# A long convolution and a SwiGLU block on one core: folded transforms, spectra kept on chip, transposes by DMA

## The chip, the core and the metric

The kernel runs on one core of a Trainium2 chip. The core has TensorE (PE, matrix products), VectorE (DVE), ScalarE (ACT), GpSimd (POOL) and SyncE (SP, here only a queue of DMAs), each with its own list of instructions that it takes in order; they meet through semaphores. 16 DMA engines move data between HBM and SBUF. The metric is the device time of one execution in microseconds (us), lower is better. Before the change it is 398.52 us, the median of three runs (397.84 to 399.33).

## The reference

The input has 2048 rows (time) of 640 channels, in bf16. Layer A is a gated long convolution, layer B a SwiGLU feed-forward block with 1728 hidden channels, each with a layer norm ahead and a residual:

```python
    k_shift = sum_t k_pad[:, t:t + S, :] * shift_k[:, ks - 1 - t]     # 4 taps
    kv = k_shift * v
    y = causal_conv(kv, ssm_k)          # rfft of length 2S, product, irfft; 2048 taps a channel
    y = y + kv * ssm_D
    A = q * y                           # q = layernorm(x)
    h = x + A
    g = silu(layernorm(h) @ w_gate);  u = layernorm(h) @ w_up
    out = h + (g * u) @ w_down
```

(`causal_conv` stands for the three FFT lines of the reference.)

## The kernel before, in words

Time is cut into four blocks of 512 rows. The convolution of a block is done by a real transform of 1024 coefficients (512 cosines, 512 sines at odd half frequencies), held as a matrix of constants: the transform is a matrix product on PE. A spectrum is a tile of 128 partitions x 8 x 640 (8 coefficient tiles; 0 to 3 the cosine half, 4 to 7 the sine half).

- `g_piece(p)` loads 512 taps of the filter (640 channels on partitions), transposes them on PE (L196) through PSUM, copies them out (L197), transforms them (`fwd_transform`, L153, 64 products of 128x128 by 320 columns, and eight copies L155), and for p > 0 combines piece p with piece p-1 by sign vectors (`hbuild`, L179 and L181). The combined spectra of p = 1 to 3 go to DRAM (`hf_dram`), and so do the raw ones of p = 1 and 2 (`graw_dram`); `pair` fetches the first kind again.
- `conv_front_tiles(j)` loads 128 rows of x, of k at four shifts and of v on SP's queue, takes the sum and the sum of squares of x on ACT (L124, L125), and computes `kv` on DVE (L257 to L262, eight operations of 640 columns per 128 rows). `conv_front_finish` normalises x on ACT (L139) and transforms `kv` into `Xcur` (64 products, L153).
- `pair(j, pp)` multiplies `Xcur` by the filter spectrum pp and adds it into the accumulator of block j+pp: six or eight DVE operations of 2560 columns (`cmac`, L162 to L176). There are ten pairs.
- `conv_back(j)` makes the inverse transform (L303, 64 products), multiplies by the normalised x (L306), adds x (L313, loaded a second time), stores h to DRAM, takes the statistics of h, normalises it on ACT (L139), transposes it on PE (L335) and copies it into `hlnT` (L336).
- `ffn_quarter(q)` runs over 14 chunks of 128 hidden channels: five products of 512 columns for the gate (L356), five for the up part (L358); ACT takes the sigmoid (L360), and copies gate (L362) and up (L364) out of PSUM; DVE multiplies twice (L366, L367). Then `ps_mm<-wd_sb,tT` (L376, 112 products of 320 columns) and, per 128 rows, the residual (L381) from h, which POOL's queue loads again, and the store. The weights of gate and up come in groups of two chunks on POOL's queue (L346, L348) for every quarter.
- `ln_finish_block` forms 1/std by an ACT square root (L134) and a DVE reciprocal (L135).

The Tile layer turns this program into one list per engine. It orders each list by the priority of the instructions (their place in the program if nothing else is said) and by its own estimate of when operands are there, and sets the semaphore waits. So the filter pieces, the front of the next block and the feed-forward block of the last one are interleaved on each engine; once built, each list is fixed.

## Time and profile before

| what | us |
|---|---|
| median of three runs | 398.52 |
| span of the profiled execution, first to last instruction | 397.7 |
| PE busy (share) | 325.7 (82%) |
| DVE busy | 254.7 (64%) |
| ACT busy | 253.8 (64%) |
| POOL busy | 68.1 (17%) |
| first product of the convolution starts at | 25.9 |
| last feed-forward block starts at about | 346 |

The profiled execution is one execution of the same program; its span lies 0.8 us under the median of the runs, and the difference is what lies around the first and last instruction. In the views, L12 is line 12 of the kernel; `out<-in xN | busy, mean` gives the busy time of a group in us and the mean of one instruction in ns; what stands behind the second bar is the idle time of the engine before the group and what ended it. A row of a timeline starts with its start and its length in us. "PEclk" is the clock that the throttle granted to PE, 1.00 being full.

### The profile page before, as it was taken

The numbers are of one execution on the slowest core, as the hardware profiler recorded it, in microseconds if no ns is written. First come the engines' busy times: TensorE is split into PE (matmuls) and PEld (weight loads), VectorE is DVE, ScalarE is ACT, GpSimd is POOL, SyncE is SP. The second block draws the span as 40 slices with busy tenths as digits, with TensorE's granted clock in tenths as the row PEclk, the third lists the DMA queues.
The fourth block names the chain that finished last, engine by engine and source line by source line (L and its number), as shares of the span: only waits on it lengthen the run. The fifth ranks groups of instructions, "written<-read, shape, count | busy, mean of one in ns | idle before, by whom it ended". The sixth has DMA issues, their size and how long they took to land.

```text
span 397.7 us, 5429 instructions
## 1 busy us (share of the span) xinstructions
PE 325.7 (82%) x1914; PEld 185.3 (47%) x1936; DVE 254.7 (64%) x413; ACT 253.8 (64%) x447; POOL 68.1 (17%) x95
## 2 busy tenths in 40 slices
PE   1038874497899779999779899897998999999995
PEld 1025542364567324565354355454534554544463
DVE  1185498500629989999949999983699723233321
...
GB/s 249 180 314 357 296 146 242 157 66 109 321 303 259 356 335 218 101 178 220 305 190 101 266 49 199 104 155 56 16 141 106 112 96 77 100 155 142 52 51 49
DMA packets 33610, 68.91 MB, mean 173 GB/s; under 512 B 4213, under 2 KB 25904, under 8 KB 31920
## 3 DMA queue, kind: packets, MB, share of 16 engines
...
HBM read 56.77 MB, written 11.80 MB: 172 GB/s over the span
## 4 chain that ended last, share of the span: by engine, by line
PE 33%; issue 25%; ACT 14%; DMA 13%; DVE 11%; SPq 2%; POOL 2%; POOLq 0%; DVEq 0%; ACTq 0%
PE ps_g L356 11%; PE ps_mm L376 7%; PE ps_mm L153 6%; PE ps_u L358 6%; PE ps_mm L303 4%; DMA wu_g<-in_B_w_up_dram 3%; ACT gc L362 3%; ACT xln_blk L139 3%; DMA k_148<-in_A_k_dram 2%; DMA wg_g<-in_B_w_gate_dram 2%; ACT junk L124 2%; SPq L250 2%; ACT sig L360 2%; DMA WF_t<-const_wf 1%; DMA wbig<-in_A_shift_k_dram 1%
## 5 line engine op out<-in xcount | busy, mean ns | idle before, releaser
L356 PE MATMUL ps_g<-hlnT,wg_g 128*128 128x512 bf16 (+1 forms) x268 | 70.9, 386 | 11.1 <-DMA wg_g<-in_B_w_gate_dram 6.1
L153 PEld LDWEIGHTS <-WF_t 128*128 128x128 bf16 x512 | 51.3, 101 | 48.7 <-DMA WF_t<-const_wf 13.8
L358 PE MATMUL ps_u<-hlnT,wu_g 128*128 128x512 bf16 (+1 forms) x270 | 70.3, 384 | 2.0 <-ACT uc L364 1.3
L376 PE MATMUL ps_mm<-wd_sb,tT 128*128 128x320 bf16 x448 | 69.6, 302 | 1.0 <-DVE tT L367 1.0
L360 ACT ACTIVATE sig<-ps_g 128x512 bf16<-128x512 f32 (+1 forms) x56 | 33.4, 597 | 50.0 <-PE ps_g L356 44.5
L376 PEld LDWEIGHTS <-tT 128*128 128x128 bf16 x448 | 41.9, 98 | 25.6 <-issue 7.1
L346 POOL DMA_DIRECT2D wg_g<-in_B_w_gate_dram x28 | 24.4, 873 | 168.9 <-PE ps_g L356 156.2
L153 PE MATMUL ps_mm<-gT,WF_t 128*128 128x320 bf16 x256 | 40.8, 313 | 15.1 <-DMA WF_t<-const_wf 13.5
L356 PEld LDWEIGHTS <-wg_g 128*128 128x128 bf16 (+1 forms) x280 | 27.3, 99 | 47.4 <-issue 14.7
L153 PE MATMUL ps_mm<-kv_blk,WF_t 128*128 128x320 bf16 x256 | 39.0, 307 | 6.9 <-ACT Xcur L155 3.9
L358 PEld LDWEIGHTS <-wu_g 128*128 128x128 bf16 (+1 forms) x280 | 27.5, 99 | 34.6 <-issue 3.7
L366 DVE TENSOR_TENSOR gs<-gc,sig 128x512 bf16<-128x512 bf16 (+1 forms) x56 | 23.2, 419 | 30.3 <-ACT gc L362 30.3
L364 ACT CAST uc<-ps_u 128x512 bf16<-128x512 f32 (+1 forms) x56 | 32.8, 586 | 10.8 <-DVE tT L367 3.3
L303 PEld LDWEIGHTS <-WI_t 128*128 128x128 bf16 x256 | 25.8, 102 | 17.5 <-issue 5.3
L362 ACT CAST gc<-ps_g 128x512 bf16<-128x512 f32 (+1 forms) x56 | 32.6, 582 | 0.0
L348 POOL DMA_DIRECT2D wu_g<-in_B_w_up_dram x28 | 24.4, 871 | 34.1 <-PE ps_u L358 21.5
L367 DVE TENSOR_TENSOR tT<-gs,uc 128x512 bf16<-128x512 bf16 (+1 forms) x56 | 23.2, 419 | 7.3 <-ACT uc L364 7.0
L155 ACT CAST Xcur<-ps_mm 128x640 bf16<-128x640 f32 x32 | 21.7, 693 | 9.0 <-PE ps_mm L153 9.0
L124 ACT ACTIVATE junk<-h_t,zero_t 128x640 bf16<-128x640 bf16 x16 | 13.2, 828 | 21.8 <-DVE h_t L313 21.5
L261 DVE TENSOR_TENSOR kv_blk<-kv_blk,ktmp 128x640 bf16<-128x640 bf16 x48 | 23.4, 487 | 0.8
L124 ACT ACTIVATE junk<-x_t,zero_t 128x640 bf16<-128x640 bf16 x16 | 13.3, 831 | 13.0 <-DMA x_t<-in_A_q_dram 12.7
L382 POOL DMA_DIRECT2D out_dram<-o_t x16 | 8.8, 553 | 65.4 <-DVE o_t L381 52.0
(256 smaller groups left out, 412.7 us busy)
## 6 DMA issues: line engine op xcount, KB each, us to landing
wg_g<-in_B_w_gate_dram POOLq DMA_DIRECT2D x24, 320.0 KB, 3.6
wu_g<-in_B_w_up_dram POOLq DMA_DIRECT2D x24, 320.0 KB, 4.2
Hld_129<-hf_dram SPq DMA_DIRECT2D x3, 1280.0 KB, 5.5
Hld_130<-hf_dram SPq DMA_DIRECT2D x3, 1280.0 KB, 9.9
gst<-in_A_ssm_k_dram SPq DMA_DIRECT2D x4, 640.0 KB, 7.7
x_t<-in_A_q_dram SPq DMA_DIRECT2D x16, 160.0 KB, 5.4
v_t<-in_A_v_dram SPq DMA_DIRECT2D x16, 160.0 KB, 3.9
h_dram<-h_t SPq DMA_DIRECT2D x16, 160.0 KB, 2.7
```

What stands on the lines that cost most here:

```text
L124: nc.scalar.activation(junk[:], x_tile, ACT.Identity, bias=zero_t[:], scale=1.0, accum_out=mv_out[:, 0:1])
L153: nc.tensor.matmul(ps[:, h, 0:NH], lhsT, src4[:, kt, h * NH:(h + 1) * NH], start=(kt == 0), stop=(kt == TT_PER_BLK - 1))
L261: nc.vector.tensor_add(ks, ks, tmp[:])
L303: nc.tensor.matmul(ps[:, h, 0:NH], lhsT, Acc[:, ct, h * NH:(h + 1) * NH], start=(ct == 0), stop=(ct == NCT - 1))
L346: nc.gpsimd.dma_start(out=wg_g[:, :, 0:ncols], in_=B_w_gate[:, f0:f0 + ncols].rearrange("(kt p) f -> p kt f", p=P))
L348: nc.gpsimd.dma_start(out=wu_g[:, :, 0:ncols], in_=B_w_up[:, f0:f0 + ncols].rearrange("(kt p) f -> p kt f", p=P))
L356: nc.tensor.matmul(ps_g[:csz, :], wg_g[:, kt, off:off + csz], hlnT[:, kt, :], start=(kt == 0), stop=(kt == 4))
L358: nc.tensor.matmul(ps_u[:csz, :], wu_g[:, kt, off:off + csz], hlnT[:, kt, :], start=(kt == 0), stop=(kt == 4))
L360: nc.scalar.activation(sig[:csz, :], ps_g[:csz, :], ACT.Sigmoid)
L362: nc.scalar.copy(gc[:csz, :], ps_g[:csz, :])
L364: nc.scalar.copy(uc[:csz, :], ps_u[:csz, :])
L376: nc.tensor.matmul(ps_o[:, h, 0:NH], lhsT, wd_sb[:csz, c, h * NH:(h + 1) * NH], start=(c == 0), stop=(c == NFCH - 1))
```

## The change

The program is written anew; what is computed stays, up to rounding. Part by part:

- **Folded transforms.** A block of 512 rows is split about its centre: rows 256 to 511 in order, and rows 255 to 0 backwards. Sum and difference of `kv` on the two halves (`xeo`, four tiles of 128 rows) are transformed by a basis of 256 rows (`WX`), cosine-like rows from the sum and sine-like ones from the difference: 32 products in place of 64. The inverse makes an even part `pe` and an odd part `po` for 256 rows (32 products in place of 64); their sum and difference are the two halves. The filter pieces keep the full transform (64 products each). With the phase taken from the centre, `hbuild` is a plain sum and a difference (`tensor_add`, `tensor_sub`) without sign vectors.
- **Row order.** The backward half is gathered: `load_rows(half=1)` issues two indirect DMAs of 128 rows on POOL's queue with a table of row numbers (`idx`); the forward half is one DMA of 256 rows on SP. Output rows of the backward half are scattered by an indirect DMA from POOL.
- **Spectra in SBUF.** G0 to G3, one more for H1, X and A live in named slots of one pool; nothing of them goes to DRAM. x stays in SBUF and becomes h in place; h is neither stored nor loaded again.
- **Transposes by DMA.** The filter pieces come from DRAM by `dma_start_transpose` (four of 640 x 512) and the normalised h by sixteen of 128 x 640, all on SP's queue. The PE transposes and their ACT copies are gone.
- **SiLU.** ACT computes SiLU out of PSUM in one step (L310 of the changed kernel) and copies the up part; one DVE product instead of two. Gate and up have two PSUM buffers each instead of one. The weights move to SP's queue.
- **Layer norm.** 1/std is a power of -0.5 in small POOL operations (seven per chain, twelve chains); the normalisations run on DVE as `tensor_scalar` instead of on ACT.
- **Order.** `prio(n)` sets the priorities by hand.

```diff
+    i = np.arange(256) + 0.5
+    wx = np.concatenate([np.cos(np.outer(i, pe)), np.sin(np.outer(i, po)),
+                         np.sin(np.outer(i, pe)), np.cos(np.outer(i, po))], axis=1)
...
+    def load_rows(dst, t, j, half, shift=0):
+        if half == 0:
+            r0 = j * MB + 256 - shift
+            nc.sync.dma_start(out=dst, in_=t[r0:r0 + 256, :].rearrange("(m p) d -> p m d", p=P))
+            return
+        for m in range(2):
+            edge = j == 0 and m == 1 and shift > 0
+            if edge:
+                nc.gpsimd.memset(dst[96:128, m, :], 0.0)
+            nc.gpsimd.indirect_dma_start(out=dst[:, m, :], out_offset=None, in_=t[:, :],
+                                         in_offset=icol(j, 2 + m, shift), bounds_check=S_TOT - 1,
+                                         oob_is_err=False)
...
+    early = big.tile([P, NF * MB], BF16, name="tT")
+    WG = early[:, 0:4096].rearrange("p (a b) -> p a b", a=4)
+    gTx = big.tile([P, NF, D], BF16, name="wd")
+    gT = [gTx[:, 0:4, :], gTx[:, 4:8, :], gTx[:, 8:12, :],
+          early[:, 4096:4096 + 2560].rearrange("p (a b) -> p a b", a=4)]
...
+            prio(p_calc + 50 * half)
+            for jj in range(4):
+                nc.vector.tensor_mul(ks[jj][:], ks[jj][:], w4[:, jj:jj + 1, :].to_broadcast([P, 2, D]))
+            nc.vector.tensor_add(ks[0][:], ks[0][:], ks[1][:])
+            nc.vector.tensor_add(ks[2][:], ks[2][:], ks[3][:])
+            nc.vector.tensor_add(ks[0][:], ks[0][:], ks[2][:])
+            nc.vector.tensor_mul(ks[0][:], ks[0][:], v[:])
+            kv.append(ks[0])
+        xeo = front.tile([P, 4, D], BF16, name="xeo")
+        nc.vector.tensor_add(xeo[:, 0:2, :], kv[0][:], kv[1][:])
+        nc.vector.tensor_sub(xeo[:, 2:4, :], kv[0][:], kv[1][:])
+        return xeo
...
+    def x_transform(j, xeo):
+        for ct in (0, 1, 6, 7, 2, 3, 4, 5):
+            odd = 2 if ct in (2, 3, 4, 5) else 0
+            ps = psA.tile([P, 2, 512], FP32, name="ps")
+            for kt in range(2):
+                for h in range(2):
+                    nc.tensor.matmul(ps[:, h, 0:NH], WX[:, kt, ct * P:(ct + 1) * P],
+                                     xeo[:, odd + kt, h * NH:(h + 1) * NH], start=(kt == 0), stop=(kt == 1))
+            nc.scalar.copy(r3(X[j][:, ct, :]), ps[:, :, 0:NH])
...
+    def hbuild(p):
+        g, gp, d = G[p], G[p - 1], H[p]
+        nc.vector.tensor_add(d[:, 0:4, :], g[:, 0:4, :], gp[:, 4:8, :])
+        nc.vector.tensor_sub(d[:, 4:8, :], g[:, 4:8, :], gp[:, 0:4, :])
...
+        e = nc.gpsimd
+        mm = small.tile([P, n, 2], FP32, name="mm" + tag)
+        e.tensor_scalar(mm[:], mv, 1.0 / D, 0.0, op0=ALU.mult, op1=ALU.add)
+        sq = small.tile([P, n, 1], FP32, name="sq" + tag)
+        e.tensor_tensor(sq[:], mm[:, :, 0:1], mm[:, :, 0:1], op=ALU.mult)
+        e.tensor_tensor(sq[:], mm[:, :, 1:2], sq[:], op=ALU.subtract)
+        e.tensor_scalar(sq[:], sq[:], 1.0, EPS, op0=ALU.mult, op1=ALU.add)
+        rs = small.tile([P, n, 1], FP32, name="rs" + tag)
+        e.tensor_tensor(rs[:], sq[:], mhalf[:, 0:n, :], op=ALU.pow)
+        nb = small.tile([P, n, 1], FP32, name="nb" + tag)
...
+        rs, nb = ln_finish(mv[:], 4, "1")
+        xln = front.tile([P, 4, D], BF16, name="xln")
+        for q in range(4):
+            nc.vector.tensor_scalar(xln[:, q, :], x[:, q, :], rs[:, q, :], nb[:, q, :], op0=ALU.mult, op1=ALU.add)
...
+        for m in range(2):
+            pe = psA.tile([P, 2, 512], FP32, name="ps")
+            for h in range(2):
+                for ct in range(4):
+                    nc.tensor.matmul(pe[:, h, 0:NH], WI[:, ct, m * P:(m + 1) * P],
+                                     A[:, ct, h * NH:(h + 1) * NH], start=(ct == 0), stop=(ct == 3))
+            es = rot.tile([P, D], FP32, name="es")
+            nc.scalar.copy(r3(es[:]), pe[:, :, 0:NH])
+            po = psA.tile([P, 2, 512], FP32, name="ps")
+            for h in range(2):
+                for ct in range(4, 8):
+                    nc.tensor.matmul(po[:, h, 0:NH], WI[:, ct, m * P:(m + 1) * P],
+                                     A[:, ct, h * NH:(h + 1) * NH], start=(ct == 4), stop=(ct == 7))
+            mv = small.tile([P, 2, 2], FP32, name="mv2")
+            for s in range(2):
+                q = m + 2 * s
+                y = rot.tile([P, D], BF16, name="y")
+                if s == 0:
+                    nc.vector.tensor_add(r3(y[:]), r3(es[:]), po[:, :, 0:NH])
+                else:
+                    nc.vector.tensor_sub(r3(y[:]), r3(es[:]), po[:, :, 0:NH])
+                nc.vector.tensor_mul(y[:], y[:], xln[:, q, :])
+                nc.vector.tensor_add(x[:, q, :], x[:, q, :], y[:])
+                stats(x[:, q, :], mv[:, s, :])
+            rs, nb = ln_finish(mv[:], 2, "2")
+            for s in range(2):
+                q = m + 2 * s
+                hl = rot.tile([P, D], BF16, name="hl")
+                nc.vector.tensor_scalar(hl[:], x[:, q, :], rs[:, s, :], nb[:, s, :], op0=ALU.mult, op1=ALU.add)
+                nc.sync.dma_start_transpose(hT[:, :, q * P:(q + 1) * P], hl[:])
...
+                sg = rot.tile([P, MB], BF16, name="sg")
+                nc.scalar.activation(sg[:z, :], pg[:z, :], ACT.Silu)
+                uc = rot.tile([P, MB], BF16, name="uc")
+                nc.scalar.copy(uc[:z, :], pu[:z, :])
+                nc.vector.tensor_mul(tT[:z, c * MB:(c + 1) * MB], sg[:z, :], uc[:z, :])
...
+        for m in (2, 3, 0, 1):
+            ps = psA.tile([P, 2, 512], FP32, name="ps")
+            for c in range(NF):
...
+            o = rot.tile([P, D], BF16, name="o")
+            nc.vector.tensor_add(r3(o[:]), ps[:, :, 0:NH], r3(x[:, m, :]))
+            if m < 2:
+                r0 = j * MB + 256 + m * P
+                nc.sync.dma_start(out=oo[r0:r0 + P, :], in_=o[:])
+            else:
+                nc.gpsimd.indirect_dma_start(out=oo[:, :], out_offset=icol(j, m), in_=o[:], in_offset=None)
...
+    prio(0)
+    nc.sync.dma_start_transpose(gT[0], A_ssm_k[:, 0:MB])
     nc.sync.dma_start(out=Drow[:], in_=A_ssm_D.partition_broadcast(1))
+    nc.scalar.dma_start(out=wb, in_=A_shift_k.partition_broadcast(P))
+    nc.scalar.dma_start(out=WG, in_=WG_h.ap())
+    nc.scalar.dma_start(out=WX[:], in_=WX_h.ap())
+    for p in range(1, 4):
+        nc.sync.dma_start_transpose(gT[p], A_ssm_k[:, p * MB:(p + 1) * MB])
+    xin[0] = load_x(0)
+    nc.sync.dma_start(out=WI[:], in_=WI_h.ap())
+    prio(100)
+    for jj in range(4):
+        nc.vector.tensor_copy(w4[:, jj, :], wb[:, :, jj])
+    nc.vector.tensor_add(gT[0][0:1, 0, :], gT[0][0:1, 0, :], Drow[0:1, :])
+    xeo[0] = conv_front(0, 10, 200)
+    prio(400)
+    g_transform(0)
+    X[0], A[0] = sp("X0"), sp("A0")
+    x_transform(0, xeo[0])
+    pair(0, 0)
+    xln[0] = x_norm(xin[0])
+    hT[0] = inverse(A[0], xin[0], xln[0])
+    prio(2000)
...
+    XS = {1: "A0", 2: "X0", 3: "A0"}
+    AS = {1: "A1", 2: "G1", 3: "A1"}
+    for j in range(NB):
+        z = 10000 * (j + 1)
+        if j + 1 < NB:
+            n = j + 1
+            prio(z)
+            xin[n] = load_x(n)
+            xeo[n] = conv_front(n, z - 5000, z)
+            if n == 2:
+                A[3] = sp("A1")
+                pair(0, 3)
+            X[n] = sp(XS[n])
+            x_transform(n, xeo[n])
+            if n == 1:
+                A[1] = sp("A1")
+                pair(0, 1)
+            pair(n, 0)
+            xln[n] = x_norm(xin[n])
+            hT[n] = inverse(A[n], xin[n], xln[n])
+            prio(z + 3000)
+            if n == 1:
+                A[2] = sp("G1")
+                pair(0, 2)
+                pair(1, 1)
+            elif n == 2:
+                pair(1, 2)
+                pair(2, 1)
+        tT[j] = ffn_up(j, hT[j], z + 5000, z - 1000)
+        ffn_down(j, tT[j], xin[j], z + 6000, z - 500)
```

Line numbers below are those of the changed kernel. Three places show how the lists moved. First, SP's queue at the start of the program, before (`gst` is the filter piece, `wbig` the taps of the short filter, `k_...` the shifted rows of k):

```order
L70 DMA ident<-const_ident 128x128
L74 DMA wbig<-in_A_shift_k_dram 128x2560
L90 DMA gst<-in_A_ssm_k_dram 128x5x512
L99 DMA sgn_t<-const_sgn 128x1
L101 DMA nsgn_t<-const_nsgn 128x1
L107 DMA Drow<-in_A_ssm_D_dram 1x640
L242 DMA x_t<-in_A_q_dram 128x640
L252 DMA k_140<-in_A_k_dram 128x640
L250 DMA k_142<-in_A_k_dram 127x640
L250 DMA k_145<-in_A_k_dram 126x640
L250 DMA k_148<-in_A_k_dram 125x640
```

and the same queue now (`wd` and `tT` are big tiles that hold the transposed filter until the feed-forward block needs them):

```order
L343 DMA_TRANSPOSE wd<-in_A_ssm_k_dram 128x4x640
L344 DMA Drow<-in_A_ssm_D_dram 1x640
L349 DMA_TRANSPOSE wd<-in_A_ssm_k_dram 128x4x640 x2
L349 DMA_TRANSPOSE tT<-in_A_ssm_k_dram 128x4x640
L109 DMA x<-in_A_q_dram 128x2x640
L99 DMA idx<-const_idx 128x32
L109 DMA k_123<-in_A_k_dram 128x2x640
L109 DMA k_125<-in_A_k_dram 128x2x640
L109 DMA k_127<-in_A_k_dram 128x2x640
L109 DMA k_129<-in_A_k_dram 128x2x640
```

The four filter pieces now stand ahead of everything that the first block needs, the row numbers for POOL included; the short filter and the two bases went to ACT's queue. The build gives the eight DMAs issued first on SP and ACT a semaphore each, and the ninth and later ones (x, idx, the k rows) wait until the DMA that had the semaphore before has landed.

Second, POOL's list around the first layer norm, now (before, POOL has only weight loads, `h` loads and stores there):

```order
L115 DMA k_156<-in_A_k_dram,idx 128x640
L115 DMA v<-in_A_v_dram,idx 128x640 x2
L225 ISA
L225 TENSOR_SCALAR mm_339<-mv_326 128x8
L115 DMA k_736<-in_A_k_dram,idx 128x640
L227 TENSOR_TENSOR sq_341<-mm_339 128x4
L115 DMA k_736<-in_A_k_dram,idx 128x640
L228 TENSOR_TENSOR sq_341<-mm_339,sq_341 128x4
L229 TENSOR_SCALAR sq_341<-sq_341 128x4
L231 TENSOR_TENSOR rs_345<-sq_341,mhalf 128x4
```

The gathers of block 0 stand ahead of the first layer norm's chain, and gathers of block 1 in its middle. The row `ISA` reloads POOL's library; there is none between compute instructions before.

Third, DVE's list while the first feed-forward block runs (`A_831` is the accumulator of block 1, `G_980` that of block 2, `tT<-sg,uc` the product of one chunk), before:

```order
L366 TENSOR_TENSOR gs<-gc,sig 128x512
L169 TENSOR_TENSOR Tprod<-Xcur,Acc_124 128x2560
L367 TENSOR_TENSOR tT<-gs,uc 128x512
L170 TENSOR_TENSOR Acc_125<-Acc_125,Tprod 128x2560
L366 TENSOR_TENSOR gs<-gc,sig 128x512
L171 TENSOR_TENSOR Tprod<-Xcur,Acc_124 128x2560
L367 TENSOR_TENSOR tT<-gs,uc 128x512
```

and now:

```order
L313 TENSOR_TENSOR tT<-sg,uc 128x512
L205 TENSOR_TENSOR A_831<-A_831,T 128x2560
L202 TENSOR_TENSOR G_980<-X_270,G_98 128x2560
L313 TENSOR_TENSOR tT<-sg,uc 128x512
L206 TENSOR_TENSOR T<-A_782,G_96 128x2560
L313 TENSOR_TENSOR tT<-sg,uc 128x512
L207 TENSOR_TENSOR A_831<-A_831,T 128x2560
```

Before, one wide operation stands between two chunk operations, and a chunk has two; now a chunk has one operation and there are one or two wide ones between chunks. From the place where block 1 is transformed on, DVE's list holds, up to the sum and difference for block 2, 22 wide operations, all 14 chunk products, five front operations and the two sums, twelve operations of the inverse, four normalisations and three residuals. PE's list has the inverse of block 1 inside the first feed-forward block (after its fifth, and in its eighth, chunk).

491 lines of the change are left out of this document (165 added, 326 removed).

## The prediction

> **What bounds the kernel now.** I read the page's first two parts, then busy time by stretch, then PE's timeline and waits.
>
> ```profile
> span 397.7 us, 5429 instructions
> PE 325.7 (82%) x1914; PEld 185.3 (47%) x1936; DVE 254.7 (64%) x413; ACT 253.8 (64%) x447; POOL 68.1 (17%) x95
> ...
> PE   1038874497899779999779899897998999999995
> PEld 1025542364567324565354355454534554544463
> DVE  1185498500629989999949999983699723233321
> ```
>
> The second part of the page gives the busy tenths of 40 slices. PE is nearly empty for two slices and nearly full from the eleventh on. DVE is full only in the middle.
>
> ```profile
> core 0: us, PE busy (x) PEld busy (x) DVE busy (x) ACT busy (x) POOL busy (x), PEclk, DMA share, GB/s
> 0.00:26.00 26.00, 2.71 (x21) 2.12 (x22) 9.25 (x22) 7.01 (x13) 5.51 (x11) 1.00 0.71 233
> 26.00:130.00 104.00, 82.69 (x552) 54.72 (x558) 55.93 (x92) 77.04 (x131) 2.85 (x4) 0.90 0.67 230
> 130.00:190.00 60.00, 54.13 (x301) 28.32 (x303) 57.67 (x81) 38.06 (x73) 13.70 (x18) 0.94 0.68 234
> 190.00:262.00 72.00, 62.09 (x353) 33.40 (x356) 65.99 (x107) 56.29 (x99) 14.66 (x19) 0.98 0.53 174
> 262.00:346.00 84.00, 77.21 (x448) 43.27 (x454) 49.91 (x83) 52.19 (x92) 18.34 (x26) 0.97 0.32 95
> 346.00:397.70 51.70, 46.91 (x246) 23.44 (x247) 15.92 (x33) 23.20 (x42) 13.04 (x18) 0.98 0.28 86
> ...
> PE ps_mm L153 <- DMA WF_t<-const_wf: 13.5, 1, 13.5
> PE ps_tr L335 <- ACT hln_t L139: 13.0, 5, 8.5
> PE ps_tr L196 <- DMA gst<-in_A_ssm_k_dram: 9.4, 2, 7.7
> ```
>
> The start costs 26 us in which PE works 2.7; then PE has 54 of 60, 62 of 72 and 77 of 84 us. Between 130 and 262 DVE is busier still (123.7 of 132): PE and DVE bound it together, PE alone at the end. PE's longest waits (cause, total, times, longest) are on the start's DMAs and on the normalised h.
>
> **What the change takes from PE.** The prices are start-to-start times in PE's timeline:
>
> ```profile
> 41.55 6.68 PE L153 MATMUL ps_mm<-kv_blk,WF_t 128*128 128x320 bf16 x48 [0.15 <-ACT Xcur L155]
> ...
> 337.80 8.08 PE L376 MATMUL ps_mm<-wd_sb,tT 128*128 128x320 bf16 x56
> ...
> 347.58 1.24 PE L356 MATMUL ps_g<-hlnT,wg_g 128*128 128x512 bf16 x5
> 348.65 1.24 PE L358 MATMUL ps_u<-hlnT,wu_g 128*128 128x512 bf16 x5
> ...
> 349.98 1.24 PE L356 MATMUL ps_g<-hlnT,wg_g 128*128 128x512 bf16 x5
> ...
> L196 PE MATMUL ps_tr<-ident,gst 128*128 128x128 bf16 x80 | 8.7, 263 | 13.5 <-DMA gst<-in_A_ssm_k_dram 9.4 <-ACT gT L197 4.0
> L335 PE MATMUL ps_tr<-ident,hln_t 128*128 128x128 bf16 x80 | 8.2, 242 | 13.3 <-ACT hln_t L139 13.0
> ```
>
> A product of 320 columns costs 6.68/48 = 0.139 us, in the down part 8.08/56 = 0.144; a chunk of ten products of 512 columns 349.98 - 347.58 = 2.40. A feed-forward block is 14 x 2.40 + 112 x 0.144 = 49.7 us, as before. Folding removes 128 products from the forward and 128 from the inverse transforms: 256 x 0.139 = 35.6 us. The PE transposes were 8.7 + 8.2 = 16.9. PE goes from 326 to about 273 us: 4 x 49.7, 256 filter products (35.6), 128 forward and 128 inverse (35.6).
>
> **What it does to DVE.** One row for each width:
>
> ```profile
> L172 DVE TENSOR_TENSOR Acc_127<-Acc_127,Tprod 128x2560 bf16<-128x2560 bf16 x3 | 4.5, 1485 | 0.0
> L261 DVE TENSOR_TENSOR kv_blk<-kv_blk,ktmp 128x640 bf16<-128x640 bf16 x48 | 23.4, 487 | 0.8
> L366 DVE TENSOR_TENSOR gs<-gc,sig 128x512 bf16<-128x512 bf16 x52 | 21.6, 419 | 27.6 <-ACT gc L362 27.6
> L306 DVE TENSOR_TENSOR h_t<-ps_mm,xln_blk 128x640 bf16<-128x640 f32 x16 | 13.0, 818 | 2.5 <-PE ps_mm L303 2.3
> L179 DVE SCALAR_TENSOR_TENSOR Acc_125<-Acc_124,sgn_t,Acc_125 128x2560 bf16<-128x2560 bf16 x1 | 2.9, 2884 | 10.9 <-DMA graw_dram<-Acc_125 10.9
> ```
>
> For 1280 columns I take 0.82 us, on the line between 0.487 at 640 and 1.485 at 2560. `tensor_scalar` on 640 columns has no row; it lies between half (0.24) and all (0.49) of the 640 row, and I take 0.45, the nearer to the row seen. The new list is: 78 operations of 2560 (72 in the pairs, six for `hbuild`, which took 2.88 each) 115.6; 72 of 1280 (the front) 59.0; 37 of 640, 18.0; 32 with PSUM 26.2; 32 `tensor_scalar` 14.4; 56 chunk products 23.4. Sum 256.6 us. DVE had 254.7: it saves the second chunk product (23 us) and half of `hbuild`, and takes over the normalisations from ACT. So **PE drops by 53 us to DVE's level, and DVE stays where it was**. In before, 130 us passed before the feed-forward blocks filled PE, and DVE had idle time there; now DVE's 247 us that precede the last feed-forward block must fit ahead of its 49.7. ACT gains eight copies of the even parts and loses far more (transposed tiles, normalisations, one of three steps a chunk, all but two of 15 table loads), so it stays behind both and out of the sum.
>
> **The start**, up to the first `xeo`:
>
> ```profile
> wg_g<-in_B_w_gate_dram POOLq DMA_DIRECT2D x24, 320.0 KB, 3.6
> gst<-in_A_ssm_k_dram SPq DMA_DIRECT2D x4, 640.0 KB, 7.7
> h_dram<-h_t SPq DMA_DIRECT2D x16, 160.0 KB, 2.7
> k_1020<-in_A_k_dram SPq DMA_DIRECT2D x1, 160.0 KB, 2.1
> ...
> 12.31 8.11 DMA k_148<-in_A_k_dram
> ...
> 20.44 0.38 SPq L386 DMA_DIRECT2D WF_t<-const_wf  x1
> ...
> L346 POOL DMA_DIRECT2D wg_g<-in_B_w_gate_dram x28 | 24.4, 873 | 168.9 <-PE ps_g L356 156.2 <-PE ps_mm L303 9.4 <-issue 3.4
> L382 POOL DMA_DIRECT2D out_dram<-o_t x16 | 8.8, 553 | 65.4 <-DVE o_t L381 52.0 <-DVE ln_msq L131 10.0 <-DMA v_t<-in_A_v_dram 3.4
> L249 POOL MEMSET k_142<- 1x640 bf16 x1 | 0.6, 621 | 0.3 <-POOLq L420 0.3
> L420 POOL MEMSET const-float32-0.0<- 128x1 f32 x1 | 0.1, 103 | 0.2 <-issue 0.2
> L155 ACT CAST Xcur<-ps_mm 128x640 bf16<-128x640 f32 x32 | 21.7, 693 | 9.0 <-PE ps_mm L153 9.0
> L134 ACT ACT_TABLE_LOAD x7 | 9.0, 1283 | 0.1
> ```
>
> The eight DMAs issued first (four filter transposes of 640 KB, the short filter 640, two bases 1024 and 512) are 4.85 MB; at the 233 GB/s of the first stretch 20.8 us. Transposes have no row. The nearest is `gst`, a plain load of the same 640 KB (7.7 us to landing beside other loads), and I price them so, by bytes; the bounds of a piece are 2.1 us (the fastest landing of the lower row) and four times the 8.11 us that the 125-row load of 160 KB took, 32 us.
>
> The Trainium skill's page "Advanced Engine Details and Errata", section X-Bar Transpose (TRN2), says that transposing DMAs are as fast as regular ones; by it the 20.8 us stay. Its page "VectorE: DVE Perf Modes", section The three transpose paths, gives 1309 ns for a 128x128 tile by DMA; 20 such tiles one after another would be an estimate of 26 us a piece. No run here shows which holds.
>
> Then the row numbers (0.38 issue, 2.1 landing): 23.3. Then POOL issues 14 gathers to the last of v. A gather lies between 0.55 (the store of 128 rows) and twice 0.87 (a load of 640 rows); I take 0.87, three memsets at 0.62: 37.3, landed 3 us later. Three DVE operations of 1280: `xeo` at **43**. Block 0's forward rows, G0 (64 products; its inputs are the first 2.4 MB, 10 us) and x's statistics lie under this.
>
> From there: eight copies of 0.69 after PE's 0.56, X0 at 49; five wide DVE operations and two of 1280 after the last copy, 9.0: A0 at **58**. In front of that pair DVE's list has the four `xln`, which wait for POOL's first chain: library reload, two gathers and seven small operations behind the last v. The nearest rows are 0.10 to 0.62 (memsets) and 1.28 (ACT's table load): 37.3 + 1.3 + 1.7 + 7 x 0.3 = 42.4, so `xln` is done by 45 and X0 hides it with 4 us to spare; beyond that each us is a us.
>
> **The middle, by DVE's list.** From A0 to block 1's first use of X1: 44.9 us of rows plus 2.2 for the first inverse products: **105**. Under it PE has G1 to G3 and X1 (26.7 + 5.6 from 60, ending at 93 if the first hT is there). hT0's path is 7 us of DVE steps, statistics, POOL's chain, a DVE step, and two pairs of transposes on SP behind k loads; with 3.6 us a pair (the `wg_g` row, between 2.1 and 7.7) it comes near 82, when PE's list asks for it inside G2.
>
> Feed-forward 0: DVE's 22 wide, 14 chunk, seven PSUM, seven of 1280 and the rest are 55.6 us; PE needs 49.7 + 4.5. DVE ends it: **161**.
>
> Feed-forward 1: PE's list has X2 finish after chunk 6: 161 + 5.2 + 6 x 2.4 = 180.6, then DVE has 47.5 until its last operation: **228**; the down products wait for the residuals queued behind wide operations, as in DVE's list.
>
> Feed-forward 2: PE is longer here: 49.7 + 4.5 + 5.6 = 59.8: **288**. DVE: 17.9 to `xeo` 3, X3 at 252, 14.9 for the pair, then inverse, chain and transposes about 19: hT3 at 286, just in time.
>
> Feed-forward 3: 49.7, residual 0.8, store 0.4 + 2.7, and 0.4 to the end: **342**.
>
> Two corrections to 105 through 288: DVE rows overlap (before, 268 us of rows in 254.7 busy, -5%), and where DVE was busiest it idled 6%; PE and DVE here alternate lists with waits both ways, so I take 6% of the 230 us from 58 to 288 as idle, less 9: +5. The span is then 347, the median by the same 0.8 us offset **348**.
>
> Edits at nothing: the spectra's stores and loads are gone, and of the waits on them only the 10.9 us at row L179 was long; it lay under PE's filter work, so I count no gain beyond the lists above. Weight loads on SP are covered by two groups of buffers, 2 x 4.8 us of PE work against 3.6 us to landing; without that cover each of 28 groups costs part of its 3.6. SP's list has the h transposes of the next block ahead of weights, waiting for DVE's `hl`: those weights are of the following block, so a late `hl` delays what would wait for it anyway.
>
> **Rivals.** (1) *DVE slower than its rows.* The short-filter product now reads its taps with a stride of zero over two row groups. If it ran at the pace of row L179 (2.88/2 = 1.44 us): 32 x 0.62 = 20 us, nearly all on DVE's list: **368**. Against it: the inner run is 640 dense elements, as now.
>
> (2) *POOL's chains stand behind DVE.* If each of a chain's seven steps had to wait for one wide DVE operation (1.48), a chain took 10.4 us in place of 2.1. Two chains on the path to hT0 (+17, of which 10 are under DVE's own 105) and two to hT3 (+17, 2 spare): +22, **370**. For it: DVE is full there; against it: POOL's rows in before (0.55, 0.87) read the same in DVE's full stretch, though none of them computes. The skill's "SBUF — State Buffer", section SBUF: two separate sides, says that a DVE operation with two SBUF inputs and a POOL operation that reads SBUF exclude each other for a whole instruction. That rule speaks for this rival; no row here shows it.
>
> (3) *The lists fit and PE sets everything.* If gathers cost 0.55 and DVE keeps up, PE runs from 93 without holes: 93 + 4 x 49.7 + 3 x 4.5 + 2 x 5 + 4.3: **320**. For it: DVE's rows overlap by 5%; against it: 22 wide operations between chunks.
>
> (4) *Slower than before: the four filter transposes hold SP.* x, idx, the k rows and through idx POOL stand behind them. At 32 us each the first `xeo` comes 128 - 21 = 107 us later: **455**. For it: the k_148 row shows a DMA of this queue that is far slower per byte than its neighbours; against it: `gst`. It decides from 398 - 348 = 50 us more, about 18 us a piece.
>
> **How the numbers follow.** Forecast 0.47 (334 to 364), (1) 0.13, (2) 0.12, (3) 0.15, (4) 0.13. About 0.5% (2 us) is what a measurement of this kernel can tell from no change; a time that near would be a mild (4). Faster 0.86 (all but (4)), same 0.02, slower 0.12. The range takes in (3), (1) and (2) together (390) and leaves out most of (4): 320 to 392.
>
> **What would show it.** Right: first `xeo` near 43, DVE over 90% from 105 to 228, PE full from 228, PE busy 270 to 280, DVE 245 to 260, hT transposes 2 to 4 us. Wrong: filter transposes of over 10 us each, `xln` or `hl` waiting for POOL's chain, PE waiting for hT3, the short-filter product at 1.4 us, PE with long gaps after 105.

## The result, and the profile after

The changed kernel takes **386.86 us** (median of four runs, 381.47 to 387.92), beside 398.92 for the kernel before on the same chip: a ratio of 0.9615, interval 0.9535 to 0.9695. It is faster by 12 us by the medians and by 15 by the ratio; 50 were forecast. A ratio leaves out the slower kind of run: here 387.36 and 387.92 are left out, and 386.36 and 381.47 remain. Below, what one version gains over another is the difference of their ratios times 399 us. The profiled execution is the one of 387.36, with a span of 385.5. From the first two parts of its page:

```profile
span 385.5 us, 4304 instructions
PE 284.8 (74%) x1504; PEld 152.9 (40%) x1520; DVE 237.1 (61%) x307; ACT 158.3 (41%) x314; POOL 143.4 (37%) x148
...
PE   0354042539599835999799994998857999999996
...
DVE  1014486747868549777999949769954884312121
POOL 0027838942694850024245580172832003200010
```

PE gave up 41 us of busy time and DVE 18, yet the span fell by 12 only. The engines are emptier than before, not slower at full load: in the first 18 slices (173 us) neither PE nor DVE is full for long. POOL went from 68.1 to 143.4 us.

The ends of the stages, read from the timeline of DVE (us):

| end of | forecast | after | late |
|---|---|---|---|
| first `xeo` | 43 | 54.3 | 11 |
| A0 | 58 | 74.3 | 16 |
| last residual of feed-forward 0 | 161 | 202.7 | 42 |
| of feed-forward 1 | 228 | 271.1 | 43 |
| of feed-forward 2 | 288 | 336.0 | 48 |
| of feed-forward 3 | 338.5 | 382.5 | 44 |

(The last forecast is 288 + 49.7 + 0.8; the 342 of the prediction takes in the store behind it.) From feed-forward 1 on the stages are within 5 us of the forecast (68, 65 and 46 us for 67, 60 and 50). Nearly all that is missing is lost ahead of 203 us: 16 up to A0, and 25 from A0 to the end of feed-forward 0. For the second piece, DVE's busy time and its waits in that stretch (cause, total, times, longest):

```profile
74.30:202.70 128.40, 100.72 (x537) 55.94 (x544) 94.50 (x118) 56.95 (x113) 56.65 (x55) 0.87 0.41 112
```

```profile
DVE k_1430 L161 <- DMA k_1430<-in_A_k_dram,idx: 5.5, 1, 5.5
DVE k_743 L161 <- DMA k_743<-in_A_k_dram,idx: 5.5, 1, 5.5
DVE xln L250 <- POOL nb_867 L234: 5.1, 1, 5.1
DVE k_1423 L161 <- DMA k_1423<-in_A_k_dram,idx: 4.3, 1, 4.3
DVE hl L283 <- POOL nb_399 L234: 2.3, 1, 2.3
DVE hl L283 <- POOL nb_919 L234: 2.3, 1, 2.3
DVE tT L313 <- ACT uc L312: 2.3, 3, 1.1
DVE hl L283 <- POOL nb_971 L234: 2.2, 1, 2.2
DVE k_750 L161 <- DMA k_750<-in_A_k_dram,idx: 1.7, 1, 1.7
DVE hl L283 <- POOL nb_451 L234: 1.7, 1, 1.7
```

128.4 - 94.5 = 33.9 us of idle time; 17.0 of it ends with a gathered piece of k, 13.6 with a chain of POOL (`nb` is its last step). Both are POOL's work. POOL's own timeline shows why they are late (start, duration, idle time before and what ended it):

```profile
47.20 1.00 POOL L115 DMA_INDIRECT v<-in_A_v_dram,idx  x1 [0.30 <-issue]
48.34 0.20 POOL L225 TENSOR_SCALAR mm_339<-mv_326 128x8 f32<-128x8 f32 x1
54.58 1.42 POOL L115 DMA_INDIRECT k_736<-in_A_k_dram,idx  x1 [6.03 <-DVE xeo L169]
56.03 0.75 POOL L227 TENSOR_TENSOR sq_341<-mm_339 128x4 f32<-128x4 f32 x1
...
60.49 0.19 POOL L234 TENSOR_SCALAR nb_347<-nb_347 128x4 f32<-128x4 f32 x1
61.31 1.22 POOL L115 DMA_INDIRECT k_757<-in_A_k_dram,idx  x1 [0.62 <-issue]
62.84 12.36 POOL L115 DMA_INDIRECT k_757<-in_A_k_dram,idx  x1 [0.30 <-issue]
...
104.25 9.20 POOL L115 DMA_INDIRECT k_1416<-in_A_k_dram,idx  x1 [2.59 <-DVE xeo L169]
```

Three things stand here. A gather costs 1.0 us or a little more and 0.3 until the next, not 0.87. The list is in order: the second step of the first chain (56.03) stood behind a gather for block 1 that waited until 54.3 for DVE to free its buffer, though its own operands had long been there. And single gathers stood for 12.36, 9.20, 7.86 and 9.42 us. DVE meanwhile, from its timeline:

```profile
60.72 1.51 DVE L250 TENSOR_SCALAR xln<-x,rs_345,nb_347 128x640 bf16<-128x640 bf16 x4 [3.14 <-POOL nb_347 L234]
...
70.70 1.49 DVE L213 TENSOR_TENSOR T<-X_270,G_96 128x2560 bf16<-128x2560 bf16 x1
72.10 0.82 DVE L165 TENSOR_TENSOR k_718<-k_718,v 128x1280 bf16<-128x1280 bf16 x1
72.84 1.49 DVE L214 TENSOR_TENSOR A_271<-A_271,T 128x2560 bf16<-128x2560 bf16 x1
79.84 0.82 DVE L161 TENSOR_TENSOR k_743<-k_743,w_91 128x1280 bf16<-128x1280 bf16 x1 [5.51 <-DMA k_743<-in_A_k_dram,idx]
```

The gather of 62.84 ended at 75.20, 0.87 us after DVE came to the end of its unbroken row (74.33). The other three ended 0.95 to 1.01 us after such an end (gathers done at 113.45, 130.82 and 280.84; rows at 112.44, 129.82 and 279.89). Here DVE stood in POOL's way, and then waited 5.51 us for what POOL had not issued.

### The profile page after: what moved, and what is told of

It is laid out like the page before. It is cut to its first block, busy times and chain, and to the rows that moved or that the text cites. A ratio compares the mean times of both kernels' runs of the same rounds, so it can differ in the third digit from the quotient of the medians.

```text
span 385.5 us, 4304 instructions
## 1 busy us (share of the span) xinstructions
PE 284.8 (74%) x1504; PEld 152.9 (40%) x1520; DVE 237.1 (61%) x307; ACT 158.3 (41%) x314; POOL 143.4 (37%) x148
## 5 line engine op out<-in xcount | busy, mean ns | idle before, releaser
L304 PE MATMUL pg<-hT,wg 128*128 128x512 bf16 (+1 forms) x267 | 72.7, 391 | 17.3 <-ACT sg L310 12.1
L306 PE MATMUL pu<-hT,wu 128*128 128x512 bf16 (+1 forms) x277 | 73.3, 389 | 0.2
L324 PE MATMUL ps<-wd,tT 128*128 128x320 bf16 x448 | 66.5, 304 | 4.8 <-DVE tT L313 3.8
L310 ACT ACTIVATE sg<-pg 128x512 bf16<-128x512 f32 (+1 forms) x56 | 33.7, 601 | 79.2 <-PE pg L304 62.0
L324 PEld LDWEIGHTS <-tT 128*128 128x128 bf16 x448 | 41.8, 99 | 29.8 <-issue 9.5
L177 PE MATMUL ps<-wd,tT 128*128 128x320 bf16 x192 | 35.2, 344 | 21.6 <-DVE wd L355 16.1
L304 PEld LDWEIGHTS <-wg 128*128 128x128 bf16 (+1 forms) x280 | 27.8, 101 | 51.8 <-issue 17.7
L187 PE MATMUL ps<-xeo,WX 128*128 128x320 bf16 x128 | 23.9, 330 | 26.2 <-DMA k_724<-in_A_k_dram 20.9
L177 PEld LDWEIGHTS <-tT 128*128 128x128 bf16 x256 | 27.6, 108 | 37.2 <-issue 23.6
L306 PEld LDWEIGHTS <-wu 128*128 128x128 bf16 (+1 forms) x280 | 28.1, 101 | 32.8 <-issue 2.7
L312 ACT CAST uc<-pu 128x512 bf16<-128x512 f32 (+1 forms) x56 | 33.1, 591 | 16.1 <-PE pu L306 15.5
L334 POOL DMA_INDIRECT out_dram<-o,idx x8 | 12.0, 1497 | 61.3 <-DVE o L329 54.8
L218 ACT ACTIVATE junk<-x 128x640 bf16<-128x640 bf16 x32 | 24.0, 750 | 23.1 <-DVE x L277 8.7
L219 ACT ACTIVATE junk<-x 128x640 bf16<-128x640 bf16 x32 | 24.1, 754 | 0.2
L262 ACT COPY es<-ps 128x640 f32<-128x640 f32 x8 | 5.5, 692 | 34.8 <-PE ps L259 29.5
L115 POOL DMA_INDIRECT k_757<-in_A_k_dram,idx x2 | 13.6, 6792 | 0.9 <-issue 0.9
```

The source lines that it names most:

```text
L115: nc.gpsimd.indirect_dma_start(out=dst[:, m, :], out_offset=None, in_=t[:, :], in_offset=icol(j, 2 + m, shift), bounds_check=S_TOT - 1, oo ...
L177: nc.tensor.matmul(ps[:, h, 0:NH], WG[:, kt, ct * P:(ct + 1) * P], gT[p][:, kt, h * NH:(h + 1) * NH], start=(kt == 0), stop=(kt == 3))
L187: nc.tensor.matmul(ps[:, h, 0:NH], WX[:, kt, ct * P:(ct + 1) * P], xeo[:, odd + kt, h * NH:(h + 1) * NH], start=(kt == 0), stop=(kt == 1))
L218: nc.scalar.activation(junk[:], src, ACT.Copy, accum_out=mv[:, 0:1])
L219: nc.scalar.activation(junk[:], src, ACT.Square, accum_out=mv[:, 1:2])
L304: nc.tensor.matmul(pg[:z, :], wg[:, kt, cc * P:cc * P + z], hT[:, kt, :], start=(kt == 0), stop=(kt == 4))
```

## Experiments

**Gathers, or chains?** In e1 the gathers are plain loads on POOL, in e1b on SP. These plain loads leave out the mirroring of the lower halves and block 0's three memsets. e2 leaves the chains out, with a constant in place of 1/std and one small DVE operation a chain for the offset; e3 is e1 and e2 together.

```diff
-            nc.gpsimd.indirect_dma_start(out=dst[:, m, :], ..., in_offset=icol(j, 2 + m, shift), ...)
+            r0 = max(0, j * MB + 128 - m * P - shift)
+            nc.gpsimd.dma_start(out=dst[:, m, :], in_=t[r0:r0 + P, :])   # e1; nc.sync in e1b
```

> The rows of the reversed halves of x, k and v are loaded in forward order by plain loads that POOL issues at the same place in its list, in place of gathers (so the lower half of each block is not mirrored, and the rows ahead of the sequence are not zero; the scattered stores and POOL's layer norm chains stay). Theory A, the gathers hold POOL whenever DVE runs two-input operations back to back, and the rows come late: about 357 us (350 to 366), no POOL issue over 1 us, first even/odd pair near 46 us in place of 53. Rival B, the layer norm chains on POOL are what DVE waits for: 378 to 384. Rival C, DVE's list and the PE clock set the pace whatever POOL does: 380 or more.

> The same forward loads, issued from SP's queue in place of POOL's. Theory A: 350 to 366, if SP's queue (h transposes and weights stand in it) does not hold them; if a load waits there for its buffer, up to 10 us more than the run with POOL's plain loads. Rivals B and C: 378 or more.

> POOL's layer norm chains are left out: the factor is a constant 20 and the offset one small DVE operation, so the variance is not used (ACT still sums the squares). The gathers stay. Theory A: 376 to 383, since the gathers still come late; what goes is the 7 us in which POOL does nothing before its first chain and part of 15.7 us of DVE waits for normalised x. Rival B: 367 or less. Rival C: 380 or more.

> Both edits: forward plain loads on POOL and no layer norm chains on POOL. Theory A: 345 to 355, that is, the lists of PE and DVE as forecast. Rival B: 345 to 355 as well, but then nearly all of it already without the chains alone. Rival C: 375 or more.

| | us | ratio to before (interval) | DVE's waits (us): gathered rows, plain rows, chains |
|---|---|---|---|
| after | 386.86 | 0.9615 (0.9535 to 0.9695) | 28, 13, 35 |
| e1, plain on POOL | 361.93 | 0.9084 (0.9017 to 0.9152) | none, 25, 27 |
| e1b, plain on SP | 347.33 | 0.8726 (0.8673 to 0.8779) | none, 14, 27 |
| e2, no chains | 345.61 | 0.8656 (0.8600 to 0.8712) | 19, 12, none |
| e3, neither | 339.56 | 0.8512 (0.8455 to 0.8569) | none, 18, none |

Either one taken away brings 21 to 38 us, both together 44: they are one queue, and the losses are not a sum. The largest miss of these four forecasts is e2's: with the gathers as the main cause it should have stayed at 376 to 383, and it came to 346, as the rival with the chains has it. In e2 gathers still stood 8.35, 7.75 and 9.88 us, so that long gathers alone do not make the kernel slow; the longest of the three:

```profile
176.78 9.88 POOL L115 DMA_INDIRECT k<-in_A_k_dram,idx  x1 [0.31 <-issue]
```

Without gathers and chains it is at 340, 8 us under the forecast: the lists of PE and DVE were not priced too low, POOL's was.

**The start.** The filter transposes stand ahead of x and `idx` on SP. In e6 pieces 1 to 3 go behind block 0's loads. In e5 POOL loads its library at the start (the constant -0.5 is then made by a multiplication), which also puts the first chain ahead of block 1's gathers; e7 is both; e9 is e6's order with e1b's plain loads.

```diff
-    for p in range(1, 4):
-        nc.sync.dma_start_transpose(gT[p], A_ssm_k[:, p * MB:(p + 1) * MB])
+    prio(40)
     ...                                  # idx, x and k, v of block 0
+    prio(80)
+    for p in range(1, 4):
+        nc.sync.dma_start_transpose(gT[p], A_ssm_k[:, p * MB:(p + 1) * MB])
```

> Two POOL instructions at the program's start make the constant -0.5 by a multiplication in place of a memset, so the library reload ahead of POOL's first computing instruction happens there, and block 0's whole first chain then stands ahead of block 1's gathers in POOL's list (before, the gather of k_736, which waits for DVE's L169, stood behind the chain's first step). Nothing is left out. Theory D, gathers and chains hold each other up in POOL's one list: the normalised x is ready before DVE asks, block 1's gathers come before DVE's wide run, DVE's waits between 55 and 83 us (3.1 + 5.5 + 1.7) go: 372 to 380. If the two only add their own times: no more than 3 us, 383 to 387.

> SP issues the filter transposes of pieces 1 to 3 behind block 0's loads of x, k and v, in place of ahead of them. Nothing is left out. If the start's lateness is carried to the end: first even/odd pair at 38 to 44 us in place of 53, total 370 to 378. If block 1's gathers then meet DVE's wide run anyway, or the filter products then come too late: 382 to 388.

> Both exact edits of the start: filter transposes of pieces 1 to 3 behind block 0's loads, and the library reload at the program's start. If what they gained apart (33 and 8) is one and the same lateness of block 1's gathers: 347 to 355. If it adds: 340 to 347.

> Forward loads by SP in place of the gathers (as in the run of 347 us: lower halves not mirrored), and the filter transposes of pieces 1 to 3 behind block 0's loads. If the late start alone is worth what it takes at the start and the rest of the 33 us came from where the gathers then meet DVE's runs: 335 to 340, some 10 us less than without the reorder. If the order at the start is worth about 30 us whatever loads the rows: 313 to 322.

e6: **353.61** (ratio 0.8884, 0.8821 to 0.8948), 29 us gained by the place of three DMAs (33 by the medians), far more than its forecast of 370 to 378. e5: 378.92 (0.9445, 0.9380 to 0.9509), 7 us. e7: 362.38 (0.9072, 0.9014 to 0.9129), 8 slower than e6 alone and outside both its forecasts. e9: 339.52 (0.8510, 0.8452 to 0.8568), where the same move, against e1b, is worth 9 us. SP's queue, of the changed kernel:

```profile
10.70 7.87 SPq L349 DMA_TRANSPOSE wd<-in_A_ssm_k_dram  x2
18.61 3.11 SPq L349 DMA_TRANSPOSE tT<-in_A_ssm_k_dram  x1
...
22.40 0.46 SPq L99 DMA_DIRECT2D idx<-const_idx  x1
```

and of e6, with its stretch from A0 (61.2) to the end of feed-forward 0 (172.5):

```profile
11.46 0.36 SPq L99 DMA_DIRECT2D idx<-const_idx  x1
...
17.87 11.60 SPq L353 DMA_TRANSPOSE wd<-in_A_ssm_k_dram  x2
```

```profile
61.20:172.50 111.30, 96.83 (x540) 54.53 (x541) 93.33 (x118) 56.87 (x113) 57.61 (x53) 0.92 0.44 121
```

A piece holds SP for 3 to 6 us, not 32 (part of such a length can be waiting: the 1.2 KB load of `Drow` behind the first piece reads 4.83); but `idx` goes out 11 us later for the three. In e6 the first `xeo` stands at 44.1, A0 at 61.2, the ends of the feed-forward blocks at 172.5, 239.0, 301.8 and 348.3. Of the 34 us between the two profiled spans, 13 come up to A0 and 17 from there to the end of feed-forward 0: DVE's work there is about the same (94.5 and 93.3), and its waits for gathered rows (17.0) are gone. The gather that had stood 12.36 us stands 5.53 here: a normalisation of x, with one wide input, came late and fell into DVE's row (57.23), and the gather ended 0.97 us after it began:

```profile
52.67 5.53 POOL L115 DMA_INDIRECT k<-in_A_k_dram,idx  x1 [0.30 <-issue]
```

```profile
55.83 1.49 DVE L207 TENSOR_TENSOR A<-A,T 128x2560 bf16<-128x2560 bf16 x1
57.23 0.45 DVE L250 TENSOR_SCALAR xln<-x,rs,nb 128x640 bf16<-128x640 bf16 x1
```

So 13 us at the start stood beside 30 by the end of feed-forward 0. e9 had no gathers that could meet a row, and the move brought 9. e1 says the same from the other side: its first `xeo` ends at 59.9, later than the changed kernel's, and it is 21 us faster. So in these runs a late start was dear only where gathers remained.

e7 has A0 where e6 has it (61.3), and lost 5 us by the end of feed-forward 0 and 5 in the next, with one gather of 17.62 us (e6: one of 16.80) and 18.3 us of DVE's waits for gathered rows (e6: 12.3). e5's gain of 7 does not add to e6's. What the runs suggest, without showing it step by step, is that each edit moves which operation of POOL meets which row of DVE; then part of e6's gain is a lucky order.

**What keeps a gather waiting.** Four measurements without the kernel's work: rows of DVE operations, and beside them operations of POOL. In m1 POOL's work is released as a row begins, in m2 to m4 in its middle.

> No part of the reference is computed (the output is a copy of x): eight stretches, in each of which three POOL operations start together with a run of DVE operations, after a DVE operation that both wait for. POOL: gathers of 128 rows in the first six, then three small multiplications of 128x8, then three plain loads. DVE: nothing; ten independent adds of 2560 from SBUF; a chain of ten such adds; ten one-input multiplications of 2560; twenty adds of 640 with one input in PSUM; a chain of 36 adds of 512; a chain of ten adds of 2560 (twice). If two-input adds from SBUF bar POOL from SBUF: gathers of 1.0 us alone, the first one 14 us in the two stretches of 2560 and 12 us in that of 512, near 1.0 to 2.4 beside one-input or PSUM operations; the small multiplications wait as the gathers do, the plain loads take 0.55 throughout. If a waiting gather gets in at the next boundary between two DVE operations: at most 2.5 us anywhere.

m1 contradicted this: gathers took 1.00 to 1.22 us beside every kind of row.

> No part of the reference is computed (the output is a copy of x). One gather at a time, its buffer read by DVE in the middle of an unbroken run of products and sums of 2560 (T = U*V, A = A + T), so that POOL starts it while DVE goes on, as in the kernel; four such with two-input operations alone, four with one addition from PSUM, four with one one-input multiplication some six us later; then four released by neighbouring operations. If it is the release in the middle of a run that makes a gather wait: 8 to 9 us in the first four (ten operations of 1.4 on, at the next gather's release or later), about 6 to 7 us in the next eight, ending at the operation from PSUM or with one input. If gathers get in at the next boundary here as well: 1.0 to 2.5 us everywhere, and the kernel's long waits need something that this run doesn't have.

m2: 2.00 to 2.17 us, one operation passed, and 1.15 to 1.22 for the last three. Longer waits were not to be had, so my cause was not shown. What m2 had not copied was that the kernel's neighbours on DVE rarely need one another: each begins 0.08 us before the one before it ends (the rows at 72.10 and 72.84 above), in m2 0.03 us after.

> A kernel that copies x to the output and computes nothing of the reference. DVE runs rows of products of 2560 columns with two inputs in SBUF; a product of 640 columns that reads a buffer releases an operation of POOL into that buffer, with DVE working on. In the earlier measurement each wide operation waited for the one before it (starts 1.52 us apart, 0.03 us between end and start) and a gather took 2.0 us. Here the products don't wait for one another, as in the kernel's spectrum products, where each starts 0.08 us before the end of the one before. A: eight independent products behind the gather. B: four, then a pair of which the second waits for the first. C: as A, with a plain load in the gather's place. D: as A, with a small multiplication. Theory 'a gather gets in only where one operation of DVE ends before the next begins': A about 11 us (eight products at 1.40) and up to 17 where sections run into each other, B about 7 to 8 (the fifth product and the 1 us after it). Rival 'the gather gets in at the next boundary': A and B 2.0 to 2.4. For C the first theory leaves open whether a plain load is held; the kernel before, where such rows read 0.55 and 0.87, says 0.6 to 0.9. D between 0.2 and 2 us (the chain rows of the changed kernel: 0.19 to 3.92).

The POOL timeline of m3:

```profile
13.81 2.21 POOL L93 DMA_INDIRECT g<-in_A_k_dram,idx  x1 [12.68 <-DVE r L99]
31.01 262.92 POOL L93 DMA_INDIRECT g<-in_A_k_dram,idx  x1 [14.99 <-DVE r L99]
```

The second gather stood for **263 us**, over some 180 wide operations, until DVE had nothing left. Neither number I had given (11 to 17) was near; the theory's direction was right. (The pair meant to wait for each other in B was taken apart by the order of the list, so m3 does not tell what lets POOL in.)

> A kernel that copies x to the output and computes nothing of the reference. Rows of independent products of 2560 columns on DVE, which overlap by 0.08 us; in such a row a gather stood 262.92 us, to its end. D: a small multiplication on POOL released in it, C: a plain load, B: a gather with a sum in the middle that waits for the product before and for which the next one waits (five operations, 7 us, after the release), E: a gather with an operation that has an input in PSUM in the middle (after four products, 5.6 us), A: a gather and eight products (11.3 us) to a gap. Theory 'overlapping two-input operations keep POOL's access out until one ends before the next begins or one reads PSUM': B about 7.5 to 8, E about 6.5, A about 12; a gather may now and then slip in at a boundary (2.2). D tells whether a chain's step is held as a gather is: then the first stands up to 60 us, to the end of its section; if not, 0.2 to 1.5 each. C the same for a plain load: up to 70 us or 0.6 to 0.9; the kernel before speaks for the latter. Rival 'only the length of DVE's run matters': B and E as A.

The POOL timeline of m4: section D (L112), C (L118), then rows of B, E and A:

```profile
27.23 36.58 POOL L112 TENSOR_SCALAR sm<-sm 128x8 bf16<-128x8 bf16 x3 [12.72 <-DVE r L111]
...
86.14 0.56 POOL L118 DMA_DIRECT2D g<-in_A_k_dram  x1 [13.65 <-DVE r L101]
...
168.76 6.21 POOL L95 DMA_INDIRECT g<-in_A_k_dram,idx  x1 [12.65 <-DVE r L101]
...
244.08 6.21 POOL L95 DMA_INDIRECT g<-in_A_k_dram,idx  x1 [11.75 <-DVE r L101]
...
319.40 2.00 POOL L95 DMA_INDIRECT g<-in_A_k_dram,idx  x1 [16.87 <-DVE r L101]
```

A small multiplication is held as a gather is: three of them, released one after another, took 36.58 us together, to the gap at 63.8 (the longest one 14.00). A plain load is not: 0.54 to 0.76, four times. In B the gather got in where a sum waited for the product before it (6.21; forecast 7.5 to 8), in E at the operation that reads PSUM (6.21; forecast 6.5). Both come after four products, so a fixed stay of 6 us would read the same; the 36.58 and the 262.92 speak against one. A missed its forecast (12): all three, and the first gather of B and of E, got in at the next boundary, 2.0 us, five operations after a gap; the held ones came nine after a gap or a read of PSUM. In the changed kernel the gather of 62.84 was held one operation after a normalisation, so the count is no rule, and when a gather slips in stays open.

The Trainium skill's page "SBUF — State Buffer", section SBUF: two separate sides, says that a DVE operation with two SBUF inputs and a GpSimd operation that reads SBUF exclude each other for a whole instruction. The runs agree in kind; but the wait was 263 us where one instruction took 1.5. Plain DMAs from POOL (0.54 to 0.76) were not held beside such operations, indirect ones were.

**Do the long gathers cost the time?** e10 gives POOL openings: behind a sum of the spectrum products, and once per filter pair, DVE copies one column (one input, 35 copies, 5.1 us). e11 is e6 with them.

```diff
+    def gap(t):
+        nc.vector.tensor_copy(one[:], t[:, 0, 0:1])
 ...
         nc.vector.tensor_add(As, As, T[:])
+        gap(As)
```

> The changed kernel; behind each sum of the spectrum products and the first of each filter pair DVE also copies one column (one input; about 0.1 to 0.15 us each, 45 of them, some 5 us of DVE's list). Theory 'DVE's overlapping rows keep POOL out': no gather over about 4 us any more, DVE's waits for gathered rows (some 30 us in all) and for POOL's chains (35 us) shrink, and the time falls from 387 towards the 362 that plain loads on POOL gave: 360 to 375. Rival 'the long gathers are not what costs': 387 to 392 with the copies added.

> The same copies in the kernel in which filter transposes 1 to 3 stand behind block 0's loads on SP (353.61 without them, with one gather of 16.80 us left). Theory: that gather shrinks to under 4 us and the time is 340 to 350. Rival: 354 to 360, the copies' price.

e10: 384.22 (ratio 0.9586, 0.9494 to 0.9677), no difference from the changed kernel that its interval shows; e11: 358.80 (0.8985, 0.8926 to 0.9044), 4 us over e6, the rival's value. The openings helped in part: gathers still stood 8.83 and 9.21 us in e10 (rows of the front have no copies), the gather that stood 16.80 in e6 took 4.88 in e11 (the longest there is one of x, 7.15); DVE's waits for gathered rows went from 28.3 to 23.8 and from 12.3 to 11.6, its waits for chains from 34.6 to 39.7 and from 29.5 to 30.6. So shorter waits of single gathers alone did not bring the time down; but the test is weak, since in e10 two of about 9 us remained and in e6 no wait of DVE came behind the gather of 16.80. What did bring it down was less on POOL's list: plain loads for the gathers, which cost less and are not held (e1, 21 us), no loads (e1b, another 14), no chains (e2, 38); and, in e6, an earlier start of the list.

**Versions that compute the same and ask less of POOL.** v1 loads k and v in order on SP and mirrors the product on PE, by an identity with its rows reversed; gathers are left for x alone. v2 is v1 with e5's and e6's edits. v3 moves the normalisations back in DVE's list; v4 takes x's gathers away as well.

```diff
+                for m in range(2):
+                    for h in range(2):
+                        nc.tensor.matmul(pr[m][:, h, 0:NH], J[:], ks[0][:, 1 - m, h * NH:(h + 1) * NH], ...)
+                    nc.scalar.copy(r3(ks[0][:, m, :]), pr[m][:, :, 0:NH])
```

> k and v are loaded in natural order by SP's plain loads; the lower half's product is mirrored by four products of 320 columns on PE with a reversed identity, and ACT copies it back (two copies of 640). Only x's gathers and the scattered stores stay on POOL, beside the chains. Nothing is left out. Theory D: as the run with SP's forward loads (347), plus up to 8 us for the mirror's latency: 345 to 356. If DVE's waits for the chains alone cost what the change lost: 365 or more.

> The three edits together: k and v in natural order with the mirror on PE, the library reload at the start, the filter transposes of pieces 1 to 3 behind block 0's loads. Nothing is left out. The start should give 8 to 14 us more than the natural order alone: 334 to 345. If PE then waits for the late filter pieces: 345 to 352.

> The natural order of k and v with the start's two edits, and besides: the identity that mirrors is ready only after the first filter piece's transform, so PE does that transform ahead of the mirror's products; the normalisations are placed later in DVE's list (x's right ahead of its use, h's of blocks 1 and 2 behind some spectrum products). Nothing is left out. PE's 34 us of waiting at the mirror go, A0 comes near 60 in place of 65, and part of DVE's 30 us of waits for the chains: 330 to 340. If the chains' waits only move: 340 to 346.

> x, k and v in natural order by SP's plain loads, all three mirrored on PE (x's lower half as well as the product), the identity ready after the first filter transform, the start's two edits; POOL has left the chains and the eight scattered stores. Nothing is left out. Without gathers (the one of x waited 6 and 12 us for POOL in the runs with k and v alone): 330 to 342. If x's mirror delays block 0's normalised x: up to 6 us more.

v1: 362.77 (358.87 to 366.42), between its two forecasts. v2: **346.73**, ratio 0.8666 (0.8621 to 0.8710), the best that computes the same, 13% under the kernel before and 10% under the changed one. v3: 351.82 (0.8797, 0.8759 to 0.8835): DVE's waits for chains fell from v2's 30.5 to 23.2, but a gather of x stood 11.63 us at 162.84. v4: 351.70 (0.8768, 0.8711 to 0.8826): no gather is left, and 16 more products are there. Both were forecast lower, and why they are slower than v2 is not shown. None is at e3's 340; the chains remain in all of them.

## Why the prediction was right in sign and wrong in size

Of its span (347) 38.5 us are missing: +16.3 up to A0, +25.4 from there to the end of feed-forward 0, +1.8 behind it, and -5 that it had set aside as corrections.

**"POOL issues 14 gathers ... I take 0.87"** failed, and with it the start (43 and 58 for 54.3 and 74.3). `idx` went out at 22.40 (20.8 was priced, so the transposes were nearly right) and POOL's first gather began at 25.66 (23.3). From there the gathers came 1.3 us apart or more, with memsets and a wait for a buffer between them, and the last of v was done at 48.20 instead of 37.3: 22.5 us for a term of 14.0. The 0.55 and 0.87 came from plain DMAs, which m4 shows not held. From `xeo` to A0 it took 20.0 us for 15; `xln` was done at 62.2, behind X0's last copy (61.6).

**Block 1's and later gathers had no price at all.** The middle was summed from DVE's list and PE's, and POOL's list of the same stretch, 17 gathers for the next blocks among chains (34 over the whole run), was not laid beside it. Of the 128.4 us of that stretch, 17.0 are DVE's waits for gathered rows; in e6, where they are gone, it is 111.3; forecast 103.

**"7 x 0.3" for a chain** was near in itself: 2.3 to 3.0 us where nothing holds it (93.84 + 0.19 - 91.21 = 2.82 for the first of h):

```profile
91.21 0.62 POOL L225 TENSOR_SCALAR mm_391<-mv_376 128x4 f32<-128x4 f32 x1 [8.19 <-ACT junk L219]
...
92.75 0.73 POOL L231 TENSOR_TENSOR rs_397<-sq_393,mhalf 128x2 f32<-128x2 f32 x1
...
93.84 0.19 POOL L234 TENSOR_SCALAR nb_399<-nb_399 128x2 f32<-128x2 f32 x1
```

What failed is "`xln` is done by 45 and X0 hides it": the chain stood behind a waiting gather (done at 60.7), and at every one of the twelve chains DVE, in order itself, stood idle at the instruction that needed it: 34.6 us over the run, where the forecast had 14 (6% of 230) for all idle time of DVE, less 9 for the overlap of rows.

**DVE's durations** held: 0.82 at L161 in the changed kernel's row (rival 1 is out), 1.49 for 2560 columns; busy 237.1, under the 245 to 260 given, because the rows overlap: one by one they add up to 256.4, just as the list had it (256.6). "DVE over 90% from 105 to 228" did not hold: 99.35 of 123 us. **PE's busy time** is 284.8 (forecast 270 to 280). It was longer where the granted clock was lower: 0.893 over this run, and in e6 and e9 278.0 at 0.937 and 274.0 at 0.958. By stretch (the columns are PE, PEld, DVE, ACT, POOL, then the clock) it was:

```profile
43.00:58.00 15.00, 4.29 (x18) 2.47 (x19) 9.87 (x13) 2.12 (x4) 7.72 (x8) 0.51 0.58 172
...
105.00:161.00 56.00, 42.18 (x214) 23.13 (x219) 38.97 (x41) 24.96 (x41) 27.74 (x17) 0.82 0.39 110
161.00:228.00 67.00, 62.27 (x335) 32.77 (x338) 60.38 (x75) 34.45 (x75) 29.42 (x29) 0.97 0.56 154
```

What sets the clock is not shown.

**The chunk's price** was misread and too high: the 2.40 us between 347.58 and 349.98 hold a product of the down part as well, which is priced a second time among the 112:

```profile
349.73 0.30 PE L376 MATMUL ps_mm<-wd_sb,tT 128*128 128x320 bf16 x1
```

Ten products alone take 2.15 there, and in the changed kernel 2.16 (341.54 to 343.70). So feed-forward 2 and 3 were priced 3.4 us too long each, which hid a part of what was late.

**The transposes of h** are as cheap as hoped: a median of 1.22 us of issue each, and PE waited for them once, 4.6 us in all.

```profile
L284 SPq DMA_TRANSPOSE hT<-hl x16: 1201/1218/1842, 94.5 to 331.1; - x16
```

**The rivals.** (2) named the right place, POOL's chains beside DVE's wide rows, and small operations can be held there (m4, D). But this is a small part of the 34.6 us: the three chains in which steps were held most took 4.9 to 6.1 us (from 96.44, 176.25 and 252.82), and DVE's waits at them add up to 5.4. At the others DVE mostly waited out the chain's own time or the gathers ahead of it, which the rival did not name. (4) had the right queue and the wrong price: 3 to 6 us a piece and not 32, yet this order was worth 29 us through what it set off. (3), PE sets everything at 320, was not reached even by e3. That (1) and (2) together (390) come near 387 is luck, since (1) is out; the stated range, 320 to 392, holds the time only because it took in rivals.

What stays open: which boundary of DVE's rows lets POOL in, and how much of the 44 us between the changed kernel and e3 is the length of POOL's list, how much its order, and how much the long waits. e2 and e10 speak against the last, but e10's openings reached only part of DVE's rows.
